# An FFT convolution layer with an MLP on one core: a depthwise-convolution unit moved ahead of the first Fourier stage, a finer last block, and sine tables spread over two products

## The chip, the cores and the metric

One core of one Trainium2 chip runs the whole layer in one launch. The metric is the device time of that launch in microseconds (us), as the median of the runs.

## The reference

With S = 2048 tokens and D = 512 channels, all in bfloat16:

```python
def _A_ref(q, k, v, shift_k, ssm_k, ssm_D):
    k_shift = sum over t of k_pad[:, t:t + S, :] * shift_k[:, ks - 1 - t]   # ks = 4 taps
    kv = k_shift * v
    y = irfft(rfft(kv padded to 2S) * rfft(ssm_k padded to 2S))[:S]         # causal long convolution
    y = y + kv * ssm_D
    return q * y

x = A_q
h = x + _A_ref(_layernorm(x), A_k, A_v, A_shift_k, A_ssm_k, A_ssm_D)
out = h + relu(_layernorm(h) @ B_w1) @ B_w2                                 # 512 -> 1376 -> 512
```

## The kernel before, in words

The transforms are written as two stages of matrix products with sine tables, and the order of every engine's instructions is the order in which the Python code issues them (a manual schedule: nothing reorders them afterwards). Each engine takes its instructions in that order, and semaphores tie the engines together. So an instruction that waits also holds what stands behind it on its own engine.

The engines: PE multiplies matrices into PSUM; ACT (sines, copies, ReLU, and the issue of the output DMAs), DVE (elementwise work) and POOL (integer tables, small vectors) do the rest; SP issues loads and DMA transposes.

**PSUM tiles.** `bank2` (L150) takes the next of four double-bank slots, in turn. A tile therefore waits until the tile four before it has been read out. From L683 on, the slots are given to `pz` (four banks, L639) and to four single banks for the MLP (`ps1m`, `ps2m`).

**Front.** Tokens are turned into rows by 32 PE transposes (`to_rows`, L271, transposes L278, read out by ACT L281 and DVE L283). The depthwise convolution is `taps(c, h)` (L329): 8 matmuls (L333) into one tile `pkv`, then a DVE product with v (L337) that leaves kv in `vT`. There are eight such units. `stage1` (L286) is the forward stage 1: 32 small matmuls (L294) into two PSUM tiles; with `dmul` (the filter, blocks `gb` 0 to 7) each of the two tiles is read twice, by a DVE addition (L306) and an ACT copy (L309), and the two engines alternate: the second ACT copy waits for the first DVE addition, and the second DVE addition for the first ACT copy. The loop L343 runs per block: `stage1`, then on ACT a sine of the large table (`more_sines`, L322, op L226), then `taps(gb // 2, gb % 2)`. In block 6, `taps(3, 0)` and `taps(3, 1, 1)` come ahead of `stage1`; the last argument makes the DVE product run in two halves, on one PSUM tile. Ahead of the loop DVE has `wrap13(r2)` (L313, op L220), which wraps the integer table `r2` that `more_sines(2)` and `(3)` read, and six tiny instructions (L315 to L319) that make the scale and bias of `ec_sins`. `ec_turns(0)` (POOL, L251 and L254) and `ec_wrap(0)` (DVE, L258) make the argument of four sines `ec_sins(0, r)` (ACT, L262), which form the core table of the inverse stage 2 for the first quarter of the tokens. After the loop, the transposes of `vT` (L391) need every DVE product of the taps.

**Middle.** Forward stage 1 of kv (L398), then stage 2 with the spectral product (L452 to L467; PE L431 and L441, ACT copies L421, DVE products L448), then four column means of `w1` (L476).

**Inverse stage 1.** `inv1(b, eng)` (L562) runs 16 blocks of 4 groups. Per group there is one 128x256 product of `BXs` (part 0) and two 128x128 products of `BK` (parts 1 and 2). Part 0 needs only the sums, parts 1 and 2 need the last DVE products of the pairs. `inv1_begin` (L556) issues part 0 of groups 0 and 2 of the blocks 0 and 1 ahead. Read-out is by two copies per tile (ACT L267 or DVE L269), to `BX` and `ax`. Blocks 14 and 15 have two tiles each, one for ACT, one for DVE.

**Inverse stage 2 and MLP**, by quarters q of the tokens. `inv2(q)` (L638, PE L646) needs all of `ax` and the four sines of quarter q. `gate(q)` (L631) multiplies by q and adds x on DVE (L632, L633), which gives `hT[q]`, and then has SP transpose it back (L635). `mlp1(sc)` (L651) computes 11 tiles of ReLU(h w1) (PE L658, ACT L660), `mlp2(sc)` (L664) four output tiles (PE L674, DVE L676, output DMA issued by ACT L679). Both take a hook that is called after each tile. In the kernel before:

```python
mlp1(0, lambda fc: ec_sins(2, (fc // 2,)) if fc in (1, 3, 5, 7) else None)   # L697
stats(xh[0], mv2, rstd2, 0); gate(1); lift(3); ec_turns(3)                   # L698 to L701
mlp2(0, next_norm(2))    # i = 0: ln1_stats(2); i = 2: ln1_norm(2); i = 3: ec_wrap(3)
inv2(2, psz)
mlp1(1, lambda fc: ec_sins(3, (fc // 2,)) if fc in (1, 3, 5, 7) else None)   # L715
```

`ec_turns(2)` and `ec_turns(3)` write the same buffer, so the second waits for the sines of the first.

Of the kernel before, what the change touches and what calls it, by code (L numbers as in the profile page):

```python
# [9 lines left out]
ALU = mybir.AluOpType  # L10
BF16 = mybir.dt.bfloat16
F32 = mybir.dt.float32
# [3 lines left out]
P = 128  # L16
# [40 lines left out]
def kernel(  # L57
# [13 lines left out]
    nc = tc.nc  # L71
    _, S, D = A_q.shape
    DFF = B_w1.shape[1]
    KS = A_shift_k.shape[1]
    assert S == 2048 and D == 512 and KS == 4, "kernel is specialised to S=2048, D=512, ks=4"
    NT = 16
    DC = D // P
# [7 lines left out]
    consts = pl.push("consts")  # L85
# [17 lines left out]
    def view(at, n, dt, t=E):  # L103
        return t[:, at:at + n].bitcast(dt)
# [7 lines left out]
    CH = 512  # L112
    sk = view(0, 4096, BF16).rearrange("p (c t) -> p c t", c=DC)
    kfl = view(4096, 4096, BF16).rearrange("p (c n) -> p c n", c=P)
    vT = view(8192, 4096, BF16).rearrange("p (c t) -> p c t", c=DC)
    wdiag = view(12288, 1024, BF16).rearrange("p (r j c) -> p r j c", r=DC, j=KS)
    kT = [view(13312 + 1056 * c, 1056, BF16).rearrange("p (r t) -> p r t", r=DC) for c in range(2)]
    kT += [view(1056 * c, 1056, BF16, F).rearrange("p (r t) -> p r t", r=DC) for c in range(2)]
    r2 = G[:, 0:2048].rearrange("p (a b) -> p a b", a=32)
# [19 lines left out]
    TURN = 2.0 * math.pi * SIN_SHRINK  # L139
# [10 lines left out]
    def bank2(name):  # L150
        return psum.tile([P, 2, 512], F32, tag="ps", name=name)[:]
# [29 lines left out]
    pi4 = consts.tile([P, 2], I32, name="pi4")  # L181
    nc.gpsimd.iota(pi4[:], pattern=[[0, 2]], base=0, channel_multiplier=1)
    rows4 = consts.tile([P, DC], F32, name="rows4")
# [34 lines left out]
    def wrap13(t):  # L218

        nc.vector.tensor_scalar(out=t, in0=t, scalar1=19, scalar2=19, op0=ALU.logical_shift_left, op1=ALU.arith_shift_right)  # L220

    nc.vector.tensor_single_scalar(out=tsn, in_=r2, scalar=n2c[:], op=ALU.mult)
    wrap13(tsn)

    def big_sin(out, turns, scale):
        nc.scalar.activation(out=out, in_=turns, func=ACT.Sin, scale=scale * TURN / 8192)  # L226
# [11 lines left out]
    nc.gpsimd.tensor_scalar(out=r2, in0=r2, scalar1=n2c[:], scalar2=2048.0, op0=ALU.mult, op1=ALU.add)  # L238


    k1o = consts.tile([P, 1], F32, name="k1o")
    rof = consts.tile([P, 1], F32, name="rof")
    esc = consts.tile([P, DC], F32, name="esc")
    ebi = consts.tile([P, DC], F32, name="ebi")
    core0 = c0p.tile([P, 32, P], F32R, name="core0")
    ecore = [core0[:].rearrange("p (h i s r) x -> p h i s r x", h=2, i=4, s=2)] + [None] * 3
    ecw = {0: tsn.rearrange("p a b -> p (a b)")[:, 0:1024].rearrange("p (h x) -> p h x", h=2)}
# [1 line left out]
    def ec_turns(q):  # L249
        w = ecw[q]  # L250
        nc.gpsimd.iota(w[:, 1, :].rearrange("p (i a n) -> p i a n", i=4, a=4), pattern=[[1, 4], [16, 4], [64, 32]],  # L251
                       base=4 * q, channel_multiplier=0)
        for h, off in ((0, 4096 + 2048), (1, 0)):
            nc.gpsimd.tensor_scalar(out=w[:, h, :], in0=w[:, 1, :], scalar1=k1o[:], scalar2=float(off),  # L254
                                    op0=ALU.mult, op1=ALU.add)

    def ec_wrap(q):
        nc.vector.tensor_single_scalar(out=ecw[q], in_=ecw[q], scalar=8191, op=ALU.bitwise_and)  # L258

    def ec_sins(q, rs=range(DC)):  # L260
        for r in rs:
            nc.scalar.activation(out=ecore[q][:, :, :, r // 2, r % 2, :], in_=ecw[q].rearrange("p h (i x) -> p h i x", i=4),  # L262
                                 func=ACT.Sin, scale=esc[:, r:r + 1], bias=ebi[:, r:r + 1])
# [46 lines left out]

    for h in range(4):
        to_rows(sk, h, kfl)
    wrap13(r2)  # L313
    for t, sh, op in ((0, 2, ALU.logical_shift_right), (1, 3, ALU.bitwise_and)):
        nc.vector.tensor_single_scalar(out=pi4[:, t:t + 1], in_=pi4[:, t:t + 1], scalar=sh, op=op)  # L315
    nc.vector.tensor_scalar(out=k1o[:], in0=pi4[:, 0:1], scalar1=2.0, scalar2=1.0, op0=ALU.mult, op1=ALU.add)
    nc.vector.tensor_copy(out=rof[:], in_=pi4[:, 1:2])
    for t, v in ((esc, TURN / 8192), (ebi, -0.5 * TURN)):
        nc.vector.tensor_scalar(out=t[:], in0=rows4[:], scalar1=rof[:], scalar2=v, op0=ALU.is_equal, op1=ALU.mult)  # L319
    big_sin(st[:, :, 0:64], tsn, 1)  # L320

    def more_sines(i):  # L322
        half = slice(16 * (i % 2), 16 * (i % 2) + 16)
        if i < 2:
            big_sin(st[:, half, 128:192], tsn[:, half], -1)
        else:
            big_sin(st[:, half, 64:128], r2[:, half], 1)

    def taps(c, h, each=2):  # L329
        ps = bank2("pkv")  # L330
        for i in range(2):
            for j in range(KS):
                nc.tensor.matmul(out=ps[:, i, :], lhsT=wdiag[:, 2 * h + i, j, :],  # L333
                                 rhs=kT[c][:, 2 * h + i, 16 - j:CH + 16 - j], start=(j == 0), stop=(j == KS - 1))
        for i in range(0, 2, each):
            vv = vT[:, 2 * h + i:2 * h + i + each, CH * c:CH * c + CH]
            nc.vector.tensor_tensor(out=vv, in0=ps[:, i:i + each, :], in1=vv, op=ALU.mult)  # L337


    inv3 = consts.tile([P, 2, 2, 64], F32R, name="inv3")  # L340
    inv12 = consts.tile([P, 2, 64], F32R, name="inv12")
    ones = consts.tile([P, P], F32R, name="ones")
    for gb in range(7):  # L343
        if gb == 6:
            taps(3, 0)
            taps(3, 1, 1)
            ec_sins(0, (2, 3))
        stage1(kfl, BK, gb, dmask)
        if gb < 4:
            more_sines(gb)  # L350
        if gb == 1:
            ec_turns(0)
        if gb == 3:
            ec_wrap(0)
        if gb in (4, 5):
            ec_sins(0, (gb - 4,))
        if gb < 6:
            taps(gb // 2, gb % 2)

    nc.gpsimd.memset(inv3[:].bitcast(F32), 0.0)  # L360
    nc.gpsimd.tensor_tensor(out=dpm[:, 0, :], in0=dsc[:, 0, :], in1=dsc[:, 1, :], op=ALU.add)
# [182 lines left out]

    blocks = {}

    def inv1_mm(b, i, parts, i0=0):
        g = 4 * b + i0 + i
        o = blocks[b][:, i].rearrange("p d a n -> p (d a n)")
        for part in parts:  # L550
            src = BXs if part == 0 else BK[:, part - 1]
            rhs = inv3[:].rearrange("p d a n -> p (d a n)") if part == 0 else inv12[:].rearrange("p a n -> p (a n)")
            nc.tensor.matmul(out=o if part == 0 else o[:, P * part - P:P * part], lhsT=src[:, g // 2, :, g % 2::2].rearrange("p c r -> p (c r)"), rhs=rhs,  # L553
                             start=(part == 0), stop=(part > 0), skip_group_check=True)

    def inv1_begin(b):  # L556

        blocks[b] = bank2("psi").rearrange("p b (i d a n) -> p (b i) d a n", i=2, d=2, a=2)
        for i in (0, 2):
            inv1_mm(b, i, (0,))  # L560

    def inv1(b, eng):  # L562
        n = 4 // len(eng)
        for i0, e in zip((0, 2), eng):
            if b not in blocks or i0:
                blocks[b] = bank2("psi").rearrange("p b (i d a n) -> p (b i) d a n", i=2, d=2, a=2)
                todo = [(i, (0, 1, 2)) for i in range(n)]
            else:
                todo = [(i, (0, 1, 2) if i % 2 else (1, 2)) for i in range(n)]
            for i, parts in todo:  # L570
                inv1_mm(b, i, parts, i0)
            for rho in range(2):
                copy(e, ax[rho][:, :, :, 8 * b + 2 * i0:8 * b + 2 * i0 + 2 * n],
                     blocks[b][:, 0:n].rearrange("p i d a n -> p a n (i d)")[:, rho].rearrange("p (n m) c -> p n m c", m=2))
# [9 lines left out]
    ecw[1] = xr1.rearrange("p i d -> p (i d)").bitcast(I32).rearrange("p (h x) -> p h x", h=2)  # L584
    ec_turns(1)
    for b in range(16):
        inv1(b, "AD" if b > 13 else "D" if b in (7, 9, 11, 13) else "A")
        if b == 0:
            for n in range(4):
                center(n)  # L590
            ec_wrap(1)
            ln1_stats(0)
        if b == 3:
            ln1_norm(0)
        if b in (8, 9, 10, 11):
            ec_sins(1, (b - 8,))
        if b == 11:
            load_x(1)
# [52 lines left out]
    def mlp1(sc, hook=None):  # L651
        h1T = h1b[sc % 2]
        h1s[sc] = h1T
        for fc in range(NFC):
            fsz = min(P, DFF - fc * P)
            ps1 = psm.tile([P, 512], F32, tag="ps", name="ps1m")
            for c in range(DC):
                nc.tensor.matmul(out=ps1[:fsz, :].rearrange("p (i t) -> p i t", i=4), lhsT=w1[:, c, fc * P:fc * P + fsz],  # L658
                                 rhs=hT[sc][:, :, c, :], start=(c == 0), stop=(c == DC - 1))
            nc.scalar.activation(out=h1T[:fsz, fc, :], in_=ps1[:fsz, :], func=ACT.Relu)  # L660
            if hook is not None:
                hook(fc)
# [31 lines left out]
    ln1_norm(1, xr1)  # L694
    load_x(3)
    lift(2)
    mlp1(0, lambda fc: ec_sins(2, (fc // 2,)) if fc in (1, 3, 5, 7) else None)  # L697
    stats(xh[0], mv2, rstd2, 0)  # L698
    gate(1)
    lift(3)  # L700
    ec_turns(3)  # L701

    def next_norm(q):
        def hook(i):
            if i == 0:
                ln1_stats(q)
            if i == 2:
                ln1_norm(q)
            if i == 3 and q == 2:
                ec_wrap(3)  # L710
        return hook

    mlp2(0, next_norm(2))
    inv2(2, psz)
    mlp1(1, lambda fc: ec_sins(3, (fc // 2,)) if fc in (1, 3, 5, 7) else None)  # L715
    stats(xh[1], mv2, rstd2, 1)
    gate(2)
    mlp2(1, next_norm(3))
# [39 lines left out]
```

## Time and profile before

| | us |
|---|---|
| median of 3 runs (210.71 to 210.79) | 210.75 |
| the profiled execution, its own time | 210.65 |
| its span in the trace | 208.9 |
| PE busy, share of the span | 197.8 (95%) |
| DVE busy | 141.3 (68%) |
| ACT busy | 116.8 (56%) |
| POOL busy | 70.0 (33%) |

The granted TensorE clock is full in all 40 slices of the span. Times in the profile are us from the span's start; "L333" is line 333 of the kernel. A row of the timeline is: start, length, engine, line, operation, what it writes and reads, shape, how many in a row; in brackets, how long the engine had been idle before it and what ended that. The chain of waits goes back from the last instruction, at each step to what released it; its rows are start, length, what. "issue" in it is time for which the profile shows no cause; in this kernel that is often the wait of a PE weight load or the delay of a semaphore.

### The profile page before, as it was taken

The numbers are of one execution on the slowest core, as the hardware profiler recorded it, in microseconds if no ns is written. First come the engines' busy times: TensorE is split into PE (matmuls) and PEld (weight loads), VectorE is DVE, ScalarE is ACT, GpSimd is POOL, SyncE is SP. The second block draws the span as 40 slices with busy tenths as digits, with TensorE's granted clock in tenths as the row PEclk, the third lists the DMA queues.
The fourth block names the chain that finished last, engine by engine and source line by source line (L and its number), as shares of the span: only waits on it lengthen the run. The fifth ranks groups of instructions, "written<-read, shape, count | busy, mean of one in ns | idle before, by whom it ended". The sixth has DMA issues, their size and how long they took to land.

```text
span 208.9 us, 4331 instructions
## 1 busy us (share of the span) xinstructions
PE 197.8 (95%) x1735; PEld 137.5 (66%) x1735; DVE 141.3 (68%) x244; ACT 116.8 (56%) x188; POOL 70.0 (33%) x118
## 2 busy tenths in 40 slices
PE   8689999988999999999999999999999999999991
PEld 3375554977899999799998944457444844444450
DVE  5978997699588989997743676987088742261131
ACT  5788777688677778677692059302960065026300
POOL 7964603980366599231003030722002100002000
PEclk9999999999999999999999999999999999999999
DMA  5999970000700000038415999999806705110011
GB/s 151 352 212 189 194 126 2 3 5 4 269 3 0 3 0 3 0 100 104 88 26 161 223 210 210 173 161 119 114 12 127 142 24 100 30 54 20 0 50 50
DMA packets 47819, 19.91 MB, mean 95 GB/s; under 512 B 42711, under 2 KB 46265, under 8 KB 47801
## 3 DMA queue, kind: packets, MB, share of 16 engines
q1 hardware_dynamic: 44144, 16.15, 41.2%
q10 hardware_dynamic: 3656, 3.51, 6.0%
q8 instruction: 13, 0.21, 0.4%
q14 instruction: 6, 0.04, 0.1%
HBM read 7.02 MB, written 2.10 MB: 44 GB/s over the span
## 4 chain that ended last, share of the span: by engine, by line
PE 83%; DVE 5%; ACT 5%; DMA 4%; issue 1%; SPq 0%; DVEq 0%; ACTq 0%
PE ps2m L674 18%; PE ps1m L658 14%; PE psi L553 11%; PE u L431 8%; PE us L441 8%; PE ps L294 8%; PE pkv L333 7%; PE pz L646 5%; DMA E<-in_A_ssm_k_dram 4%; PE pst L278 3%; ACT BX L262 2%; DVE st L511 1%; ACT M L660 1%; DVE qT L632 1%; DVE BK L448 1%
## 5 line engine op out<-in xcount | busy, mean ns | idle before, releaser
L660 ACT ACTIVATE M<-ps1m 128x512 bf16<-128x512 f32 (+1 forms) x44 | 25.0, 601 | 50.0 <-PE ps1m L658 39.6
L674 PE MATMUL ps2m<-M 128*128 128x512 bf16 (+3 forms) x187 | 38.8, 367 | 0.0
L674 PEld LDWEIGHTS <-M 128*128 128x128 bf16 (+1 forms) x187 | 18.2, 98 | 20.1 <-ACT M L660 0.4
L658 PEld LDWEIGHTS <-w 128*128 128x128 bf16 (+1 forms) x176 | 17.4, 100 | 20.4 <-issue 0.7
L381 POOL TENSOR_TENSOR smc<-st 64x256 fp32r<-64x256 f32 x32 | 22.8, 731 | 15.8 <-PE us L441 15.0
L515 POOL TENSOR_SCALAR rstd<-mv 128x4 f32<-128x4 f32 x8 | 2.2, 276 | 70.4 <-DVE mv L513 70.4
L676 DVE SCALAR_TENSOR_TENSOR M<-ps2m,rstd,M 128x512 bf16<-128x512 f32 (+1 forms) x13 | 9.2, 707 | 24.0 <-PE ps2m L674 15.5
L448 DVE TENSOR_TENSOR BK<-u,ktu 128x512 fp32r<-128x512 f32 x32 | 20.6, 685 | 4.9 <-PE us L441 2.7
L553 PE MATMUL psi<-inv,BX 128*128 128x256 f32 x64 | 21.5, 341 | 0.2
L553 PE MATMUL psi<-inv,BK 128*128 128x128 f32 x128 | 21.6, 254 | 0.0
L421 ACT COPY ktu<-u 128x512 f32<-128x512 f32 x32 | 18.0, 588 | 5.2 <-DVE BK L448 2.4
L553 PEld LDWEIGHTS psi<-inv,BK 128*128 128x128 f32 x128 | 20.1, 197 | 0.0
L658 PE MATMUL ps1m<-xT,w 128*128 128x512 bf16 (+1 forms) x88 | 19.6, 379 | 0.2 <-ACT M L660 0.2
L658 PE MATMUL ps1m<-M,w 128*128 128x512 bf16 (+1 forms) x88 | 19.3, 380 | 0.0
L431 PE MATMUL u<-BK,st 64*128 64x256 f32 x128 | 14.2, 303 | 0.1
L431 PE MATMUL u<-BX,st 64*128 64x256 f32 x128 | 13.0, 284 | 0.0
L553 PEld LDWEIGHTS psi<-inv,BX 128*128 128x128 f32 x64 | 12.4, 197 | 0.7 <-DVE BK L448 0.7
L309 ACT CAST BK<-ps 128x512 fp32r<-128x512 f32 x16 | 9.4, 585 | 6.2 <-PE ps L294 4.0
L511 DVE BATCH_NORM_STATS2 st<-M 128x6 f32<-128x512 bf16 x20 | 12.3, 676 | 0.0
L632 DVE TENSOR_TENSOR qT<-pz,qT 128x2048 bf16<-128x2048 f32 x2 | 4.6, 2292 | 10.9 <-DMA qT<-M 6.8
L337 DVE TENSOR_TENSOR E<-pkv,E 128x1024 bf16<-128x1024 f32 (+1 forms) x9 | 9.9, 1104 | 2.7 <-PE pkv L333 2.7
L441 PE MATMUL us<-BK,smc 128*128 128x256 f32 x64 | 10.8, 294 | 0.7 <-ACT BX L267 0.6
(126 smaller groups left out, 403.5 us busy)
## 6 DMA issues: line engine op xcount, KB each, us to landing
E<-in_A_ssm_k_dram SPq DMA_DIRECT2D x1, 2048.0 KB
out_dram<-M ACTq DMA_DIRECT2D x15, 128.0 KB
w<-in_B_w_dram SPq DMA_DIRECT2D x1, 1376.0 KB
M<-in_B_w_dram ACTq DMA_DIRECT2D x1, 1280.0 KB
M<-in_A_q_dram SPq DMA_DIRECT2D x8, 128.0 KB
xh<-in_A_q_dram SPq DMA_DIRECT2D x4, 128.0 KB
xr<-in_A_q_dram SPq DMA_DIRECT2D x4, 128.0 KB
out_dram<-M ACTq DMA_DIRECT2D x2, 64.0 KB
```

The source lines that it names most:

```text
L294: nc.tensor.matmul(out=pss[rp][:, gi // 2, :, gi % 2, :], lhsT=fl[rows, 2 * g:2 * g + 2, :].rearrange("p d n -> p (d n)"), rhs=f[rows].rea ...
L333: nc.tensor.matmul(out=ps[:, i, :], lhsT=wdiag[:, 2 * h + i, j, :], rhs=kT[c][:, 2 * h + i, 16 - j:CH + 16 - j], start=(j == 0), stop=(j = ...
L381: nc.gpsimd.tensor_tensor(out=smc[pq, c % 3, i, :, 64 * dp:64 * dp + 64], in0=st[pq, ks, 64:128].bitcast(F32), in1=st[pq, ks, 0:64].bitcas ...
L421: nc.scalar.copy(out=kt[:], in_=ps)
L431: nc.tensor.matmul(out=ps[:, dp, 256 * x:256 * x + 256], lhsT=t[pq], rhs=cols((BK, BX)[x], pq, k1, i), start=(i == 0), stop=(i == 1), tile ...
L441: nc.tensor.matmul(out=ps[:, k % 2, 256 * x:256 * x + 256], lhsT=smc[:, k // 4 % 3, i, k % 4, :], rhs=cols((BK, BX)[x], slice(0, P), k, i) ...
L448: nc.vector.tensor_tensor(out=o, in0=ps[:, :, 256:512].rearrange("p b (g x) -> p b g x", x=8), in1=kt[:].rearrange("p b (g x) -> p b g x", ...
L511: nc.vector.bn_stats(out=st[:, i, :], in_=src[:, i, :])
L553: nc.tensor.matmul(out=o if part == 0 else o[:, P * part - P:P * part], lhsT=src[:, g // 2, :, g % 2::2].rearrange("p c r -> p (c r)"), rh ...
L658: nc.tensor.matmul(out=ps1[:fsz, :].rearrange("p (i t) -> p i t", i=4), lhsT=w1[:, c, fc * P:fc * P + fsz], rhs=hT[sc][:, :, c, :], start= ...
L660: nc.scalar.activation(out=h1T[:fsz, fc, :], in_=ps1[:fsz, :], func=ACT.Relu)
L674: nc.tensor.matmul(out=ps2, lhsT=h1T[:ksz, fc, i * P:(i + 1) * P], rhs=w2[:ksz, fc, d0:d0 + w], start=(fc == 0), stop=(fc == NFC - 1))
```

## The change

1. The first tap unit `taps(0, 0)` runs ahead of `stage1` block 0, and each later unit ahead of the next block (a unit moves from behind its block to in front of it).
2. `taps(3, 1, 1)` takes two PSUM tiles, one for each half, where both halves were in one.
3. On DVE, the six tiny instructions go ahead of the read-out of the first transposes, and `wrap13(r2)` goes into block 1, behind its two additions.
4. `inv1_begin` issues part 0 of all four groups of the blocks 0 and 1. The odd groups' part 0 then doesn't restart its bank.
5. Block 15 of the inverse stage 1 is read out in four tiles, by ACT, DVE, ACT, DVE.
6. The four sines of quarter 2, all in `mlp1(0)` before (after tiles 1, 3, 5, 7), stand after tiles 3 and 8 of `mlp1(0)` and, on ACT, behind the output DMAs of tiles 0 and 1 of `mlp2(0)`. `ec_turns(3)` goes from ahead of `mlp2(0)` to the hook of its tile 2, `ec_wrap(3)` behind the call of `inv2(2)` (on DVE its place is the same). The sines of quarter 3 stand after tiles 1, 4, 7, 10 of `mlp1(1)`.

```diff
     def taps(c, h, each=2):
-        ps = bank2("pkv")
-        for i in range(2):
-            for j in range(KS):
-                nc.tensor.matmul(out=ps[:, i, :], lhsT=wdiag[:, 2 * h + i, j, :],
...
-        for i in range(0, 2, each):
-            vv = vT[:, 2 * h + i:2 * h + i + each, CH * c:CH * c + CH]
-            nc.vector.tensor_tensor(out=vv, in0=ps[:, i:i + each, :], in1=vv, op=ALU.mult)
+        for r0 in range(2 * h, 2 * h + 2, each):
+            ps = bank2("pkv")[:, 0:each, :]
+            for i in range(each):
+                for j in range(KS):
+                    nc.tensor.matmul(out=ps[:, i, :], lhsT=wdiag[:, r0 + i, j, :],
...
+            vv = vT[:, r0:r0 + each, CH * c:CH * c + CH]
+            nc.vector.tensor_tensor(out=vv, in0=ps, in1=vv, op=ALU.mult)
...
     for gb in range(7):
-        if gb == 6:
+        if gb < 6:
+            taps(gb // 2, gb % 2)
+        else:
             taps(3, 0)
             taps(3, 1, 1)
             ec_sins(0, (2, 3))
...
         if gb == 1:
+            wrap13(r2)
             ec_turns(0)
...
-        if gb < 6:
-            taps(gb // 2, gb % 2)
...
     def inv1_begin(b):
...
-        for i in (0, 2):
-            inv1_mm(b, i, (0,))
+        for i in range(4):
+            inv1_mm(b, i, (0,), sums_first=True)
...
-        inv1(b, "AD" if b > 13 else "D" if b in (7, 9, 11, 13) else "A")
+        inv1(b, "ADAD" if b == 15 else "AD" if b == 14 else "D" if b in (7, 9, 11, 13) else "A")
...
-    mlp1(0, lambda fc: ec_sins(2, (fc // 2,)) if fc in (1, 3, 5, 7) else None)
+    mlp1(0, lambda fc: ec_sins(2, (fc // 6,)) if fc in (3, 8) else None)
...
-    ec_turns(3)
...
         def hook(i):
+            if i < 2 and q == 2:
+                ec_sins(2, (2 + i,))
             if i == 0:
                 ln1_stats(q)
             if i == 2:
                 ln1_norm(q)
-            if i == 3 and q == 2:
-                ec_wrap(3)
+            if i == 2 and q == 2:
+                ec_turns(3)
...
     inv2(2, psz)
-    mlp1(1, lambda fc: ec_sins(3, (fc // 2,)) if fc in (1, 3, 5, 7) else None)
+    ec_wrap(3)
+    mlp1(1, lambda fc: ec_sins(3, (fc // 3,)) if fc in (1, 4, 7, 10) else None)
```

## The prediction

> **What bounds the kernel.** I read the engine table, then the chain of waits, then the timeline around each break of the chain. PE is busy 95% of the span and carries 83% of the chain: only its pauses are worth anything, and only if nothing takes their place. The chain:
>
> ```profile
> 9.46 4.07 PE pst L278 x32
> 13.54 0.02 issue
> 13.56 0.70 DVE E L283
> ...
> 14.40 1.07 PE ps L294 x32
> ...
> 36.09 0.38 issue
> 36.47 2.94 PE pst L278 x24
> ...
> 88.13 0.69 DVE BK L448
> 88.82 0.04 issue
> 88.87 22.81 PE psi L553 x190
> 111.67 0.02 issue
> 111.70 0.43 DVE BX L269
> 112.12 0.34 DVE ax L269
> 112.46 0.14 issue
> 112.60 3.91 PE pz L646 x32
> ...
> 122.80 0.59 DVE M L258
> ...
> 123.42 1.24 ACT BX L262
> ```
>
> PE pauses at 13.54 (0.86 us), at 36.09 (0.38), before 88.87, at 111.67 (0.93), and is held by ACT's sines from 123.42 to 129.39. The change goes at all five. What it moves the last wait to is in the timeline of ACT and DVE:
>
> ```profile
> 137.57 1.37 DVE L676 SCALAR_TENSOR_TENSOR M<-ps2m,rstd,xh 128x512 bf16<-128x512 f32 x2
> 138.31 0.55 ACTq L679 DMA_DIRECT2D out_dram<-M  x1
> ```
>
> The first of these two L676 ends at 138.28; ACT then issues the output DMA of tile 1 for 0.55. In the changed kernel the sine r = 3 of quarter 2 stands directly behind this issue, and `inv2(2)`, whose first matmul came at 139.61, needs that sine.
>
> **The change, part by part** (times on before's clock; "+" is gain).
>
> *1. First unit ahead.* PE stands still 13.54 to 14.40. The unit's inputs are there: keys at 9.08 (L134, 1.79 + 7.29), tap weights at 8.70 (L204), its slot free at 11.65 (ACT L281). So 8 of its matmuls fill the hole: **+0.86**. The 0.10 that block 1 loses now (chain: 1.10, other blocks 1.00; it waits for an ACT copy that ends at 17.30) goes: +0.10. Against it: three units in a row cost 5.30 now, a lone one 1.84; with two in a row, one more is lone: 1.84 - 5.30/3 is about 0.07 to 0.11: -0.11. The six tiny DVE instructions (15.30 to 16.00, 0.70) fall into DVE's idle 0.70 ahead of 11.53; without that cover each 0.1 would go straight to PE, which already waits 0.16 there for L283.
>
> *2. Last unit in two tiles.* Now both halves' products (L337, 35.08, two in 1.29) start when all 8 matmuls are done, and the transposes wait 0.38 for them. With two tiles, the first half's product starts some 0.9 earlier, the second ends about 0.65 after the unit, while the 32 matmuls of block 6 (1.0) still run: **+0.38**. Four sines of quarter 0 now end at about 35.95 (34.63 now), because the last three follow block 5's copies one unit later; ACT's next copy then waits about 0.1, covered by the transposes that run meanwhile. POOL's tables behind them (L375, L381) start 1.3 later, the fourth at 41.8, and are first read at 52.25.
>
> *3. The wrap inside block 1.* A block takes PE 2.84 (1.00 + 1.84); DVE 2.41 (product 20.28 to 21.42 = 1.14, two additions 1.27). The wrap adds 1.13 (L220, 14.17 to 15.30), so DVE falls 0.7 behind. Who waits: block 3's second tile is freed by block 2's second ACT copy, behind block 2's first addition, behind its product, behind the wrap. DVE: product 18.34, additions 19.48, wrap 20.75, product 21.88, addition 23.02 to 23.66, ACT copy to 24.31. PE is ready for block 3 at 23.92: **-0.43**. DVE makes it up by 0.44 per block, so it is paid once. There is more: POOL's second L254 should run from 20.42 to 21.15, across the start of the wrap, and this trace shows what that does:
>
> ```profile
> 3.57 1.94 POOL L180 IOTA G<- 128x2048 int32 x1
> 3.58 1.98 DVE L44 TENSOR_SCALAR E<-E,n2c 128x64 int32<-128x64 int32 x1
> 118.92 1.23 DVE L633 TENSOR_TENSOR xT<-qT,xT 128x2048 bf16<-128x2048 bf16 x1
> 132.91 1.42 DVE L633 TENSOR_TENSOR M<-M 128x2048 bf16<-128x2048 bf16 x1
> ```
>
> The small L44 (0.25 elsewhere) took 1.98, as long as the POOL iota that began 0.01 before it; but L633, which began with 0.35 of an L254 to go, lost only 0.19. So the wrap loses between 0 and 0.40; I take 0.22, near L633's: **-0.22**.
>
> The Trainium skill ("SBUF — State Buffer", "Who interferes with whom") says the port pair that VectorE and GpSimd share is locked for a whole instruction, and whoever comes second blocks fully. L44 agrees, L633 only in part. By that rule the wrap would lose the full 0.40 and the forecast would be 0.18 less.
>
> Parts 1 to 3: 0.86 + 0.10 - 0.11 + 0.38 - 0.43 - 0.22 = +0.58.
>
> *4. Early products.* Block 0's tile comes free with the first of the last two L448 (88.13), block 1's with the second (88.82). Two products of block 0 now run at 88.27, then PE waits to 88.87. Two more fit, at the stage's pace of 22.81/190 = 0.12: **+0.24**. The two extra ones of block 1 only change places, for when they run everything is ready: 0. All of inverse stage 1 comes **0.82** earlier (0.58 + 0.24).
>
> *5. Quarters.* The last read-out is two DVE copies of 256 columns, 0.43 and 0.41, the second 0.34 behind the first; 512 columns take 0.69 and 0.68, 0.61 apart. On that line 128 columns take 0.30 and 0.28, 0.21 apart: the end is 0.49 after the start instead of 0.75: **+0.26**. Bounds: 0, if a small copy costs as much as the 256 one, and 0.38, half of it.
>
> *6. Sines.* `mlp1(0)` takes PE 10.00 (120.25 to 130.25), `mlp1(1)` 9.51 (143.48 to 152.99): 0.49 lost to sines, and 0.04 more in `mlp2(0)`. With two sines, the first behind tile 3 when `ec_wrap(2)` (123.38) is long done, ACT is never more than a tile behind (tile 10 out 10.7 after the start; its reader comes at 11.7). So PE would reach `inv2(2)` 0.82 + 0.26 + 0.53 = 1.61 earlier.
>
> But the sine r = 3 isn't ready then. Followed back: ACT's issue of tile 1, L676 of tile 1, `ln1_stats(2)` (L511, L513), L676 of tile 0, `gate(1)`, the statistics of xh0, and their data: an SP transpose (122.26 to 125.70, landed 127.69) that stood behind 7.36 of SP's issue of another (112.66) and 2.14 of loads. All of that starts from the end of inverse stage 1, not from PE's later gains: it moves by 0.82 and no more. One thing helps: POOL no longer runs `ec_turns(3)` beside L633 (1.42, then 1.23): 0.19. So: L676 138.28, issue to 138.86, sine (1.24) to about 140.15, PE 140.20; less 0.82 and 0.19: 139.19. Now the first matmul is at 139.61, and its third 0.43 behind it; at 112.60, where PE had stood still, the third came after 0.31. So 139.61 counts as about 139.70. Gain that survives: **0.51**, and PE waits about 1.1 where it never waited.
>
> Behind it nothing is late. `ec_turns(3)` starts when that sine ends (139.1), needs 0.62 + 1.48 or up to 3.03; `ec_wrap(3)` at about 142, first sine of quarter 3 wanted at about 145. Its four sines, 3 tiles apart, leave the last tile of `mlp1(1)` out 10.95 after the start, needed at 11.7. From `inv2(2)` to the end the chain is PE without a break, so it all arrives at the end.
>
> **The sum.** 210.65 (the profiled execution) - 0.51 = 210.14; the median of the runs is 0.10 above the profiled one: **210.2**.
>
> **Rivals.**
>
> *A. The sine is in time* (15%). If the transpose lands sooner, as DMA traffic shifts against it, DVE's chain is no longer last. For: L519's 7.36 is 1.9 elsewhere, so traffic decides it. Against: the two loads it shares with move along. Gain up to 1.61: **209.1**.
>
> *B. The front gives nothing* (15%). The wrap at full port price or a late read-out eats 0.4 more, everything else as forecast: gain 0.1, **210.6**.
>
> *C. Slower: the DMA issue ahead of the sine is long* (10%). Same place, other price. Of this product's four issues by ACT, two took 0.65 and 0.55, but the next two this:
>
> ```profile
> 138.97 1.76 ACTq L679 DMA_DIRECT2D out_dram<-M  x1
> 141.64 1.20 ACTq L679 DMA_DIRECT2D out_dram<-M  x1
> ```
>
> An issue of 1.06 makes the change worth nothing (0.55 + 0.51), beyond 1.48 it is slower by over 0.2%; at 1.76: 210.2 + 1.2 = **211.4**. Against: 1.76 came right behind another issue, this one stands alone.
>
> **Chances.** Forecast 60%, A 15, B 15, C 10. This measurement tells about 0.2% (0.42 us) from no change, so the forecast's 0.51 is near that bound: of its 60, 40 faster, 20 same. With A 15 faster; B 2 faster, 12 same, 1 slower; C 3 same, 7 slower: faster 0.57, same 0.35, slower 0.08. The range reaches to A at one end and half of C's way at the other, and takes in the bounds of parts 3 and 5: 209.1 to 210.9.
>
> **What the profile would show.** Part 1: the first L333 at 13.6, the first L294 about 15.4. Part 2: no wait of L278 for DVE near 36. Part 3: a pause of PE ahead of the fourth block's L294 of 0.4 to 0.8, and L220 there longer than 1.22. Part 4: four L553 near 88 without a break. Part 5: L269 rows of 128 columns at 0.3. Part 6: `mlp1(0)` in 9.5; a wait of L646 for ACT L262 of about 1.1 at `inv2(2)`. No such wait speaks for A; an L679 over 1.1 ahead of that sine, for C. I am wrong altogether if PE pauses at a place that is not named here.

## The result: slower, with a half clock and a late sine

The changed kernel takes **213.24 us** (median of 6 runs, 211.75 to 213.63) against 210.74 (210.59 to 210.79): ratio 1.0111, 95% interval 1.0081 to 1.0141. The forecast was 210.2, within 209.1 to 210.9. The profiled execution took 213.01, with a span of 210.9 and a mean granted clock of 0.987.

In some executions of either kernel the chip grants TensorE half the clock for 3.41 us (of the kernel before, 18 of 77 runs took 211.9 to 212.4 at a mean clock of 0.987 to 0.989, the others 210.4 to 211.1; of the changed kernel, 5 of 6 took 213.0 to 213.6 at 0.987 to 0.992, and one 211.75 at 0.995), so a single comparison holds luck, and the experiments below take it apart.

PE's waits in the changed kernel (line, what it waited for: total, times, longest):

```profile
PE pz L646 <- ACT BX L268: 2.1, 1, 2.1
PE pst L284 <- DMA E<-in_A_ssm_k_dram: 2.0, 1, 2.0
PE ps L300 <- ACT BK L315: 1.2, 2, 0.8
```

The first is the wait at `inv2(2)` that the prediction named, at twice its forecast 1.1. The last holds the 0.76 ahead of the fourth block. The page's clock row, one digit for each 40th of the span, shows what the prediction didn't name:

```profile
PEclk9969999999999999999999999999999999999997
```

The third slice, 10.5 to 15.8, has 6 tenths of the clock. In the chain of waits (start, length, what) the same place and the late sine read so:

```profile
9.35 5.43 PE pst L284 x32
...
21.73 1.82 DVE G L220
23.54 1.13 DVE E L337
24.67 0.61 DVE BK L312
...
25.94 1.05 PE ps L300 x31
...
88.98 23.17 PE psi L555 x192
...
126.28 5.98 DMA M<-xr
...
132.35 2.30 DVE M L632
...
139.23 0.65 DVE M L676
...
139.90 0.55 ACTq L679
...
140.49 1.25 ACT BX L268
...
141.78 3.94 PE pz L646 x32
```

The 32 transposes took 5.43 instead of 4.07: that is 1.36. Inverse stage 1 ended at 112.15, not near 110.9. `inv2(2)` began at 141.78 instead of 139.70, behind the sine r = 3, behind an issue of 0.55, L676, the statistics, and `gate(1)` (L632), whose input, the xr transposes, landed 5.98 after the start of their issue. From 141.78 on, PE runs as before, so these 2.08 arrive at the end.

### The profile page after: what moved, and what is told of

It is laid out like the page before. It is cut to its first block, busy times and chain, and to the rows that moved or that the text cites. A ratio compares the mean times of both kernels' runs of the same rounds, so it can differ in the third digit from the quotient of the medians.

```text
span 210.9 us, 4335 instructions
## 1 busy us (share of the span) xinstructions
PE 198.4 (94%) x1727; PEld 139.0 (66%) x1735; DVE 142.3 (67%) x246; ACT 117.4 (56%) x190; POOL 70.2 (33%) x118
## 4 chain that ended last, share of the span: by engine, by line
PE 73%; DMA 13%; DVE 7%; ACT 3%; issue 2%; ACTq 0%; SPq 0%; DVEq 0%
PE ps1m L658 14%; PE ps2m L674 13%; PE psi L555 11%; PE u L433 8%; PE us L443 8%; PE ps L300 7%; PE pkv L334 5%; PE pst L284 4%; DMA E<-in_A_ssm_k_dram 4%; DMA M<-in_B_w_dram 4%; PE pz L646 4%; DMA M<-xr 3%; DMA xh<-xT 2%; DVE st L513 2%; DVE E L337 1%
## 5 line engine op out<-in xcount | busy, mean ns | idle before, releaser
L676 DVE SCALAR_TENSOR_TENSOR M<-ps2m,rstd,M 128x512 bf16<-128x512 f32 (+1 forms) x13 | 9.2, 707 | 25.4 <-PE ps2m L674 16.9
L555 PE MATMUL psi<-inv,BK 128*128 128x128 f32 x128 | 21.1, 255 | 0.0
L555 PE MATMUL psi<-inv,BX 128*128 128x256 f32 x64 | 20.4, 337 | 0.1
L513 DVE BATCH_NORM_STATS2 st<-M 128x6 f32<-128x512 bf16 x20 | 12.3, 679 | 0.0
L450 DVE TENSOR_TENSOR BX<-us,kts 128x512 fp32r<-128x512 f32 x16 | 10.9, 686 | 0.8
```

Source lines behind the costliest of these rows:

```text
L450: nc.vector.tensor_tensor(out=o, in0=ps[:, :, 256:512].rearrange("p b (g x) -> p b g x", x=8), in1=kt[:].rearrange("p b (g x) -> p b g x", ...
L513: nc.vector.bn_stats(out=st[:, i, :], in_=src[:, i, :])
```

## The experiments

Three theories stood at first. **L**: the late sine and the half clock are the loss, the front's and inverse stage 1's gains came. **F**: the front moves cost by themselves. **K**: the half clock alone. Beside these runs the kernel before took medians of 210.67 to 210.76.

**old_sines** takes back part 6:

```
-    mlp1(0, lambda fc: ec_sins(2, (fc // 6,)) if fc in (3, 8) else None)
+    mlp1(0, lambda fc: ec_sins(2, (fc // 2,)) if fc in (1, 3, 5, 7) else None)
...
-            if i < 2 and q == 2:
-                ec_sins(2, (2 + i,))
```

> The changed kernel with part 6 alone taken back (sines, turns and wrap of quarters 2 and 3 as before); parts 1 to 5 stay. Theory L (the late sine r = 3 at inv2(2) costs about 2.1, the half clock in the first transposes 1.36, parts 1 to 5 bring 0.87 + 0.26 as forecast): PE doesn't wait at inv2(2), and mlp1(0) takes 10.0 again. 210.65 - 0.82 - 0.26 = 209.6 where the first transposes run at full clock, 210.9 where the half clock falls into them. Theory F (the front and the read-outs of inverse stage 1 cost by themselves, the sines were as good as forecast): 212.5 to 213.5. Theory K (the half clock alone explains the loss, the sine does no harm): 212.2 with the half clock, since the sines' own 0.5 is given back.

Measured: 209.99 (10 runs; eight at 209.8 to 210.25, two at 211.2), ratio 0.9964 (0.9937 to 0.9991); PE doesn't wait at `inv2(2)`. Theory F falls. Parts 1 to 5 bring 0.7 where no half clock comes, less than the 1.08 of theory L.

**sines_only** is the kernel before with part 6 alone, the same diff the other way.

> The kernel before with part 6 alone. Theory L: the sine r = 3 comes at 140.2 (as the prediction's chain) to 141.7 (as in the changed kernel's trace), inv2(2) starts by then instead of 139.65: 211.2 to 212.8, with a PE wait for ACT of 1 to 2.6 at inv2(2). Theory F or K (no harm in the sines): 210.2 to 210.7, the wait below 1. The clock shows whether the half clock falls into the first transposes here too; that adds 1.36 and is told apart from the sines by the transposes' time (4.07 at full clock).

Measured: 214.81 (212.54 to 215.45, 4 runs), ratio 1.0167 (1.0100 to 1.0235). Theory K falls: the sines alone cost 2 to 5, half clocks included. That is also above theory L's 211.2 to 212.8, even with 1.36 for a half clock. Its windows (from:to, length, then busy time of PE, PEld, DVE, ACT and POOL, the granted clock, DMA share, GB/s; PEld is PE's weight load) show why it is more than the pause of 2.3:

```profile
139.72:143.14 3.42, 1.31 (x11) 1.31 (x12) 2.87 (x7) 1.24 (x1) 2.18 (x3) 1.00 0.92 150
143.14:146.55 3.41, 3.41 (x19) 3.41 (x18) 2.39 (x5) 0.00 (x0) 1.01 (x2) 0.50 0.49 98
```

The pause fell into one window, and the next was granted half the clock: a pause of PE can be paid again, by up to 1.7. In the changed kernel's profile the pause of 2.14 lay across two windows, with PE busy for 2.52 and 2.17 of them, and the clock stayed.

**long_fill** has `fill(..., 30)` instead of 22 ahead of the first transposes.

> The changed kernel with 30 instead of 22 fill products ahead of the first transposes, so that PE's idle gap there is about 0.3 instead of 1.98. Theory L with the clock: no half clock in the transposes (4.1 instead of 5.43), psi ends 1.3 earlier; the sine's wait at inv2(2) grows or stays, since its chain starts from the end of inverse stage 1 and moves too: 213.2 - 1.4 = 211.8. If the gap has nothing to do with the clock: 213.2, transposes 5.4. If the sine's chain hangs on something that does not move (a load's landing): 212.6 to 213.2 at full clock.

Measured: 211.78 (nine runs at 211.2 to 213.2; one at 216.7 is not in the ratio), ratio 1.0046 (1.0013 to 1.0079). The transposes take 4.30, of which 0.28 is a wait for DVE's read-out (L289); inverse stage 1 ends at 111.28 instead of 112.15. As theory L has it; what is left over the kernel before is the sine's wait (1.7 in the profile, and a half clock behind it there). The window ahead of the transposes in three kernels, first before, then old_sines, then the changed one with the window after it:

```profile
7.78:11.19 3.41, 1.73 (x15) 1.76 (x16) 2.96 (x5) 1.76 (x6) 3.37 (x8) 1.00 1.10 263
```

```profile
7.62:11.04 3.42, 1.51 (x13) 1.55 (x14) 3.33 (x8) 3.42 (x13) 3.38 (x9) 1.00 1.08 256
```

```profile
7.41:10.82 3.41, 1.47 (x13) 1.50 (x14) 3.30 (x9) 3.41 (x13) 3.37 (x10) 1.00 1.09 286
10.82:14.24 3.42, 3.42 (x19) 3.42 (x18) 2.17 (x8) 1.68 (x3) 2.80 (x4) 0.50 1.12 201
```

The same idle gap of 1.9 to 2.05, cut differently by the window's start. With PE busy for 1.73 or 1.51 of the 3.41 the clock stayed, with 1.47 it fell. It isn't a sharp bound: behind a window with 1.69 busy, at long_fill's `inv2(2)`, it fell too. The Trainium skill ("TensorE: Matmul & The Clock Gate", "What's actually happening") says that the window is 3413 ns and runs freely; the events at 3.998, 10.824 and 14.238 agree (two windows, then one). It names an idle window as the cause; here one that was busy for 43% sufficed.

**four_ahead** is long_fill with all four sines of quarter 2 in `mlp1(0)`, so that none stands behind an output issue:

```
+    mlp1(0, lambda fc: ec_sins(2, (min(fc // 3 - 1, 2) + fc // 10,)) if fc in (3, 6, 9, 10) else None)
```

> The changed kernel with 30 fill products and all four sines of quarter 2 inside mlp1(0), behind tiles 3, 6, 9 and 10, so that none stands behind an output issue. Theory L: PE reaches inv2(2) 0.82 + 0.26 + 0.5 earlier than before and nothing is late there: 209.0 to 209.3. If another input of inv2(2) or of mlp2(0) is pinned as well (the gate's data, a tile slot held by a late ACT): 209.6 to 210.7, with the wait for it in the trace. Theory F: above 210.7.

Measured: 209.51 (209.12 to 209.75, 6 runs), ratio 0.9927 (0.9900 to 0.9955); no wait at `inv2(2)`, and PE gets there at 138.21 instead of 139.61. So the wait hangs on the sine's place. The time lies between theory L's 209.0 to 209.3 and the next range; wrap_ahead, below, finds the rest in part 3.

But why was gate(1) late? It has two inputs that come late: the statistics of xh0 (L513, L515 in the changed kernel), which the prediction followed back to the xh transposes, and the transposes of `xr`, which it didn't name. In the kernel before, SP's queue and DVE:

```profile
126.04 1.92 SPq L519 DMA_TRANSPOSE M<-xr  x1
```

```profile
130.08 0.36 DVE L513 BATCH_NORM_AGGREGATE mv<-st 128x2 f32<-128x6 f32 x4
130.59 2.29 DVE L632 TENSOR_TENSOR M<-pz,M 128x2048 bf16<-128x2048 f32 x1
```

DVE goes from the statistics to the gate almost without a gap. In sines_only the front is that of the kernel before. The same rows there:

```profile
126.19 1.92 SPq L519 DMA_TRANSPOSE M<-xr  x1
128.16 3.36 SPq L491 DMA_DIRECT2D M<-in_A_q_dram  x4
```

```profile
129.71 0.36 DVE L513 BATCH_NORM_AGGREGATE mv<-st 128x2 f32<-128x6 f32 x4
132.41 2.29 DVE L632 TENSOR_TENSOR M<-pz,M 128x2048 bf16<-128x2048 f32 x1 [2.34 <-DMA M<-xr]
```

The transposes are issued 0.15 later than before, and the statistics end 0.37 earlier, but gate(1) starts 1.8 later, and DVE stands idle for 2.34. One thing that differs on the queues there is the time of one packet on queue 8. Such packets have 16,384 bytes and come once for every 250 or so matmuls and weight loads, which fits PE's code: in all 13 profiles this one began when PE had started 2,725 to 2,750 of them. In sines_only PE is ahead in `mlp1(0)`, so the piece comes at 130.23 instead of 131.14. This is theory **C**: the piece hits the last packets of the transposes. The window 129.7 to 131.3 of sines_only has it (packets, MB, share):

```profile
q8 instruction: 1, 0.02, 3.6%
```

The Trainium skill ("Runtime: NRT & Kernel Launch", "Instruction fetch mechanics") gives blocks of 16 KiB or 256 instructions through a DMA queue of the sequencer, and calls the cost mostly hidden. The size and the spacing agree. PE didn't wait for it here (it shows no pause near 130), but another engine's transfer seems to have.

**code_later** moves the piece by the PE instruction count: the changed kernel with fewer, longer fill products (`fill32` is a product on the same zeros read as fp32).

```
-    fill(bank2("psz")[:, 0, :], 22)
+    fill(bank2("psz")[:, 0, :], 2)
+    fill32(bank2("psz")[0:64, 0, :], 7)
```

> The changed kernel, whose 22 bf16 fill products are replaced by 2 bf16 and 7 fp32 ones: about as much PE time as 30 bf16 ones (so the gap ahead of the transposes is closed as in long_fill), but 42 PE instructions fewer than in long_fill. PE's code comes in pieces of 16 KB on queue 8, one for about 256 PE instructions; at some 9 instructions per us in mlp1(0) the piece that came at 126.6 in long_fill and at 130.0 in the changed kernel should come at about 131. Theory C (this piece, falling among the packets of the xr transposes, delays their landing and with it gate(1), the first output tiles and sine r = 3): here it comes when gate(1)'s L632 is already running; L632 starts at about 129.8, sine r = 3 ends at about 139.0 and inv2(2) starts at about 139.1, waiting 0.4 instead of 1.7: 210.3 to 210.5. Rival (the landing is late for another reason, or the output issues ahead of the sine are the whole price): L632 after 130.8, inv2(2) at 140 or later, 211.3 to 211.9 as long_fill.

Measured: 210.78 (210.38 to 211.57, 10 runs), ratio 0.9999 (0.9974 to 1.0024). The piece came at 129.34, too early, 2.0 behind the end of the issue; yet L632 began at 130.12 and `inv2(2)` waited 0.8. Six runs lie at 210.4 to 210.8, four at 211.2 to 211.6. Half a confirmation at best: the profiled execution, 210.43, lies in theory C's range, but the median lies above it, and the piece's place is not theory C's.

**before_fill** is the kernel before with `fill(..., 30)`.

> The kernel before with 30 instead of 22 fill products, nothing else. Theory on the clock (the idle gap of 1.9 ahead of the first transposes, where it falls within one window of 3.41, gives half a clock for the next window and costs 1.4; that is why some runs of the kernel before take 212): all runs at 210.3 to 210.7, none near 212. Rival (the 212 runs come from elsewhere): some runs near 212 here too.

Measured: 211.00 (210.63 to 211.56, 10 runs), ratio 0.9999 (0.9975 to 1.0023). No run near 212, as expected of the clock. But not 210.3 to 210.7 either: in its profile the full clock came only at 6.59, so the longer fill ended late and the first transposes began at 10.38 instead of 9.46 (in the chain of waits). And unasked for: without any sine moved, the piece came 2.0 behind the issue's end, and L632 4.2 behind it.

**code_last** and **sines_last** push the piece further back: 7 fp32 products in place of the 22, and the two fill products behind inverse stage 1 left out, in the changed kernel and in sines_only.

> The changed kernel with 7 fp32 fill products instead of 22 bf16 ones, and without the two fill products behind inverse stage 1: 8 PE instructions fewer than code_later. Theory C (PE's 16 KB code piece delays the landing of the xr transposes when it falls where their last packets do; in code_later it came 2.0 behind the end of their issue, in sines_only 2.1, in before_fill 2.0, in the changed kernel 1.8, and it delayed three of these four; in the kernel before it came 3.2 behind, when they had landed): here it comes 2.7 to 3.2 behind; L632 starts 2.5 to 2.8 behind the end of the issue, inv2(2) waits 0.4 to 0.8, and the runs lie at 210.2 to 210.8, with none or few of the 211.2 to 211.6 that 4 of 10 runs of code_later took. Rival: the landing varies by itself: L632 4 behind in the profile, or runs at 211.2 and above as often as in code_later.

> sines_only (the kernel before with part 6 alone) with the same fill as code_last, so that only the PE instruction count ahead of mlp1(0) differs. Theory C: the code piece comes about 3 behind the end of the transposes' issue instead of 2.1, L632 at about 130.7 instead of 132.4, sine r = 3 at 140.2 as the prediction worked out, inv2(2) waits 0.6 to 0.9 instead of 2.3, no half clock behind it: 210.9 to 211.4 instead of 212.5 to 215.5. Rival: L632 at 132 again, wait of 2 or more: 212.5 and above.

Measured: code_last **210.17** (209.94 to 210.38, 10 runs), ratio 0.9960 (0.9937 to 0.9984); sines_last 210.89 (six runs at 210.8 to 210.9, four at 211.4 to 211.5, where the fill ended late as in before_fill), ratio 0.9987 (0.9961 to 1.0013). In both the piece came further back than expected (table below), and `inv2(2)` waited 0.5. In sines_last:

```profile
126.72 1.93 SPq L525 DMA_TRANSPOSE M<-xr  x1
128.69 2.39 SPq L497 DMA_DIRECT2D M<-in_A_q_dram  x4
```

```profile
131.19 2.29 DVE L637 TENSOR_TENSOR M<-pz,M 128x2048 bf16<-128x2048 f32 x1 [0.83 <-DMA M<-xr]
```

It differs from sines_only in fill products alone, and the landing is back at 2.54. All 13 profiles (the last three are of runs told below), in us behind the end of the transposes' issue:

| kernel | issue took | code piece | gate(1) starts |
|---|---|---|---|
| before | 1.92 | +3.18 | +2.63 |
| old_sines | 1.92 | +3.25 | +2.57 |
| code_last | 1.93 | +4.61 | +2.54 |
| sines_last | 1.93 | +4.79 | +2.54 |
| changed kernel | 1.93 | +1.80 | +4.14 |
| sines_only | 1.92 | +2.12 | +4.30 |
| before_fill | 1.94 | +2.02 | +4.21 |
| code_later | 1.93 | +2.01 | +2.79 |
| long_fill | 3.40 | -2.18 | +2.27 |
| four_ahead | 3.27 | -2.09 | +2.33 |
| all_mended | 1.93 | +2.26 | +2.52 |
| wrap_ahead | 3.58 | -1.53 | +2.27 |
| turns_later | 3.04 | -1.93 | +2.40 |

At +2.26 or later the piece is harmless (five of five). At +1.80 to +2.12 gate(1) starts late: by 1.5 to 1.8 in three profiles, by 0.2 in code_later. Inside the issue it stretches the issue by 1.1 to 1.7 instead (four of four), and in each of the four the piece ends 0.57 ahead of the issue's end.

The packets in the trace tell more. The transposes' data go in packets of 256 bytes. In the five harmless profiles the last of them ends at +1.86 to +1.90. In code_later, before_fill and sines_only it ends at +2.00, +2.03 and +2.12, just where the piece begins (+2.01, +2.02, +2.12), and in the changed kernel nine of them come when the piece (+1.80 to +2.73) is done, the last at +3.01. The landing is told by 16 semaphore updates: in sines_only and before_fill 15 of them came by +2.72 and +2.58, and one at +4.21 and +4.11, as if one of the 16 DMA engines had been held. In the changed kernel all 16 came late, at +3.91 to +4.05. Theory C stands, as a hit or a miss of up to 1.8; why code_later lost so little, and why in the changed kernel all 16 were late, is open.

**wrap_ahead** is four_ahead with `wrap13(r2)` ahead of the loop again.

> four_ahead with part 3 taken back: wrap13(r2) stands before the loop again, while DVE waits for the first tap unit's product. Theory: the wrap in block 1 costs PE the 0.76 pause before the fourth block's L300 (L220 took 1.83 there beside POOL's L260, the product behind it came late); ahead of the loop it costs at most 0.2, since DVE waits there from 14.4 to 15.4. Gain 0.5 to 0.8 against four_ahead: 208.7 to 209.0, no pause near 24. Rival (the pause has another cause, or the wrap only moves it to the first block): within 0.2 of four_ahead, 209.3 to 209.7.

Measured: 208.76 (208.75 to 209.10, 4 runs), ratio 0.9900 (0.9861 to 0.9939). The time is in the expected range, and the pause ahead of the fourth block is gone.

**turns_later** emits `ec_turns(0)` in block 2 instead of block 1.

> four_ahead with the wrap where the changed kernel has it, but POOL's ec_turns(0) one block later, so that no POOL instruction of it runs beside L220. If the shared port is what stretches L220: 1.22 instead of 1.83 and the PE pause shrinks by 0.5 to 0.6 to about 0.2, 208.9 to 209.1. If DVE's place in the order is the cause (the forecast's 0.43 without the port): the pause stays at 0.4 or more, 209.2 to 209.6. POOL's next work (L362 to L369) moves up beside the wrap and could stretch it as well; then L220 stays above 1.22.

Measured: 209.32 (209.25 to 210.00), ratio 0.9934 (0.9911 to 0.9957), and void: POOL has nothing else queued there and starts it when ACT's sines have read the tile (19.14 against 18.87), so nothing moved. What the port does to the wrap can only be read from rows, those of four_ahead:

```profile
20.57 1.83 DVE L220 TENSOR_SCALAR G<-G 128x2048 int32<-128x2048 int32 x1
```

```profile
19.59 1.49 POOL L260 TENSOR_SCALAR G<-G,k1o 128x512 int32<-128x512 int32 x2
...
21.29 1.28 POOL L363 TENSOR_TENSOR E<-E 128x64 f32<-128x64 f32 x1
```

L220 begins 0.5 before L260 ends and takes 0.61 longer than its 1.22; L363, 0.32 elsewhere, lasts until L220 is done. In wrap_ahead, where the two lie apart, L220 takes 1.22 and L363 0.32. This speaks for the full blocking that the prediction weighed and priced at 0.40; no run changes POOL's work alone.

**all_mended** takes the three mendings together: the wrap ahead, the four sines in `mlp1(0)`, 7 fp32 fill products.

> The changed kernel with its parts 1, 2, 4 and 5, and three mendings together: the wrap ahead of the loop (wrap_ahead), all four sines of quarter 2 in mlp1(0) (four_ahead), and 7 fp32 fill products instead of 22 bf16 ones, which end before the transposes' data land even where the full clock comes late (with 30 bf16 ones the transposes start up to 0.6 late in some runs). If the three are independent: 208.4 to 208.8 in all runs, no run above 209. If the gap of about 1.0 that is left ahead of the transposes still gives a half clock in some runs: these at 209.8 to 210.2. If the code piece, which comes later here, meets something that wrap_ahead's did not: above 209.

Measured: 208.82 (208.64 to 208.95, 4 runs), ratio **0.9908** (0.9892 to 0.9925). It is wrap_ahead's time again, a hair above the expected range: 0.9% faster than the kernel before.

## Why the prediction was wrong

**Parts 1 and 2: right, a little small.** The hole behind the transposes and the 0.38 ahead of the second ones are gone. From the first transposes to the second, by the chains of waits, it is 27.01 before (9.46 to 36.47) and 25.57 in wrap_ahead (9.79 to 35.36): 1.44 gained, forecast 0.86 + 0.10 - 0.11 + 0.38 = 1.23. Where the other 0.21 comes from is open.

**Part 3: right in mechanism, too small.** With the wrap in block 1 the same stretch is 26.52 (four_ahead, 9.57 to 36.09): 0.95 lost, forecast 0.43 + 0.22 = 0.65. The term that was mis-sized is the port's: L220 took 0.61 longer, where the prediction took 0.22 and gave 0.40 as the most. The idle time that was to hold the six tiny instructions didn't always do so: in old_sines and long_fill DVE reached the read-out behind them late, and PE waited 0.28.

**Part 4: right.** From the second transposes to the end of inverse stage 1: 75.21 before, 74.98 in four_ahead (36.09 to 87.85 + 23.22); 0.23, forecast 0.24. **Part 5: right.** From there to `inv2(0)`: 0.92 before, 0.66 in four_ahead; 0.26, as forecast; the read-outs of 128 columns took 0.29 and 0.28.

**Part 6: the step that failed is the path back from `gate(1)`.** PE's own gain was right: `mlp1(0)` takes 9.49 in the changed kernel. But the prediction followed gate(1) to one input, the statistics of xh0 and the xh transposes, and said of them: "All of that starts from the end of inverse stage 1, not from PE's later gains: it moves by 0.82 and no more." It left out the other input, the landing of the xr transposes. In the changed kernel the statistics were done at 130.27, and the landing came last:

```profile
126.28 1.93 SPq L521 DMA_TRANSPOSE M<-xr  x1
```

```profile
129.91 0.36 DVE L515 BATCH_NORM_AGGREGATE mv<-st 128x2 f32<-128x6 f32 x4
132.35 2.29 DVE L632 TENSOR_TENSOR M<-pz,M 128x2048 bf16<-128x2048 f32 x1 [2.08 <-PE ps2m L674]
```

(The bracket puts the wait down to a PE product that ended about then; the chain shows the landing.) And this landing hangs on PE after all, through the code piece that PE's progress calls for. gate(1) was forecast at 130.59 - 0.82 = 129.77 and began at 132.35, 2.58 later. Of this, 1.07 was there when the xr transposes had been issued (128.21 instead of 127.14); it goes with the half clock, by which inverse stage 1 ended late. The other 1.51 is the landing. From gate(1) to `inv2(2)` the chain was worked out rightly: 139.19 - 129.77 = 9.42 forecast, 141.78 - 132.35 = 9.43 measured. The two add up: 210.14 + 2.58, and 0.28 more outside the span, are the 213.0 of the profiled execution; and the one run at a clock of 0.995, 211.75, lies 1.5 above the forecast, as the landing alone would have it. Where neither falls in, in code_last, `inv2(2)` began at 139.02 and the kernel takes 210.17; the forecast was 139.19 and 210.2. PE waited 0.53 there instead of about 1.1, as PE itself came later than forecast.

**What the sum didn't hold at all is the clock.** The prediction read a full clock in all 40 slices and took it as given, and it didn't name PE's longest pause, the 1.91 ahead of the first transposes:

```profile
9.46 4.06 PE L278 MATMUL pst<-identw,E 128*128 128x128 f32 x32 [1.91 <-DMA E<-in_A_ssm_k_dram]
```

By their mean clock, a quarter of the runs of the kernel before pay for a pause; the three shown ahead of the prediction were not among them. That it is this one is borne out by the eight kernels whose profiles show at most 0.96 there and no pause over 0.8 at `inv2(2)` (before_fill, code_later, code_last, sines_last, four_ahead, wrap_ahead, turns_later, all_mended): none of their 63 runs has a mean clock under 0.994. How long the gap is depends on the clock as well. The fill products ahead of it start 0.43 apart until the full clock is granted, at 4.36 in the kernel before, and 0.22 apart from then on, which the page's row of nines doesn't show; in sines_only, with the same front, the full clock came at 6.60, and the gap was 0.97. Whether the changed kernel is more prone to it (5 of 6) is open: its code up to there differs in DVE only, and old_sines, with the same front, paid in 2 of 10. Its wait at `inv2(2)` is a second place, where long_fill and sines_only were hit, and only one of the five was profiled.

**The rivals.** C ended on the right side by the wrong cause: the issue ahead of the sine took 0.55, as in the forecast. A looked at the right kind of thing, a landing that traffic moves, but at other transposes, and it moved the other way. The price of a miss there was never worked out.

## What to carry to other kernels

Putting work on an engine behind a chain that ends late leaves PE's start at the mercy of every link, each DMA landing among them; price the chain's worst link before counting the gain, or keep the work where only PE's own pace sets it. In this kernel a gap of PE near 2 us was a coin tossed for 1.4 to 1.7 more, at the gap's end; close such a gap or count it. Changing how many instructions PE has run by some point moves its code loads, and here they landed on a transfer that was needed.

## What was not expected of the hardware

- PE's code comes as 16,384 bytes on queue 8 for about 250 matmuls and weight loads; when it fell 1.8 to 2.1 behind the end of a transpose's issue, what waited for that transpose started 0.2 to 1.8 later (four of four profiles; none of five at 2.26 or later), and when it fell into the issue, the issue took 3.0 to 3.6 instead of 1.92 (four of four).
- One idle stretch of 1.7 to 2.3 us cost 3.41 us at half the clock (transposes 5.43 instead of 4.07) or nothing, and how the window's edge cut it bears on that: with PE busy for 1.31, 1.47 or 1.69 of the window the clock fell, with 1.51, 1.73, 2.17 or 2.52 it stayed.
